# Pacing the row gathers of a mixture-of-experts kernel behind its first-layer results

## The chip, the cores and the metric

The kernel runs on one core of one Trainium2 chip. The metric is the device time of one execution, in microseconds. Engines are called as the profile calls them: PE is TensorE (the matrix engine, PEld its weight loads), DVE is VectorE, ACT is ScalarE, POOL is GpSimd, SP is SyncE. POOL also issues the indirect DMAs, which fetch or store rows by a list of row numbers.

## The reference

Attention over channels gives 20224 tokens of 256 numbers; each token then goes to one of eight experts, with a fixed capacity, best logits first; each expert is a two-layer network.

```python
def _attn_ref(q, k, v, tau):            # B, N, C = 4, 5056, 256
    qn = q / (np.linalg.norm(q, axis=1, keepdims=True) + 1e-06)
    kn = k / (np.linalg.norm(k, axis=1, keepdims=True) + 1e-06)
    s = kn.transpose(0, 2, 1) @ qn / tau
    s = s - s.max(-1, keepdims=True)
    a = np.exp(s)
    a /= a.sum(-1, keepdims=True) + 1e-09
    return (v @ a).astype(np.float32)

def _moe_ref(x, w_gate, w1, w2):        # N, D, E, F = 20224, 256, 8, 1024
    cap = N // E
    order = np.argsort(-(x @ w_gate).flatten())
    for idx in order:                   # greedy: best logits first
        tok, e = (int(idx) // E, int(idx) % E)
        if assigned[tok] >= 0 or counts[e] >= cap:
            continue
        assigned[tok] = e
        counts[e] += 1
...
    for e in range(E):
        mask = assigned == e
        h = np.maximum(x[mask] @ w1[e], 0.0)
        out[mask] = h @ w2[e]
    return out
```

## The kernel before

The first part (to about 340 us) computes the attention and writes its rows x to a table in device memory, x_d. The rest is the expert part, which the change touches. It runs in eight phases p, one expert each. Which tokens the expert gets is found by a routing search on DVE, with small matmuls on PE (L508 and L521 fill pc; DVE answers in Dm and Ex, L511 and L517), which runs one phase ahead beside the matmuls. It ends in a list of row numbers per expert (src to gather, idx to scatter).

An expert's 2528 tokens stand in 20 columns of up to 128, cut into chunks (p, c) of up to four columns: five chunks of 4, or for the first expert 2, 4, 4, 4, 4 and 2. A chunk goes through these steps:

- **Gather** (`load_x`, L1002): per column one indirect DMA on POOL's queue, 128 rows of 1 KB from x_d to the buffer xg, of which there are three. `load_x` only puts the gathers into a Python list, `queue`; `gather()` issues the next one from it. It is called after every unit of layer 1 and every column of layer 2. The gathers of chunk c + 3 are put into the list when chunk c has been turned.
- **Turn** (`turn`, kb = 0 and 1, L1029): PE transposes half the channels of up to four columns into the PSUM buffer pt, ACT copies them to xH (L1031), DVE takes the rest in xL (L1034).
- **Layer 1** (`layer1`): eight units fb, each of six matmuls (L1064: two halves, times the pairs of a high and a low part) into one of three PSUM buffers ph; ACT writes hH with the Relu (L1067), DVE writes hL (L1072). hH and hL have two buffers each, so a chunk's are written again two chunks later.
- **Layer 2** (`layer2`): per column 24 matmuls (L1095) into py, ACT copies to y (L1100), POOL writes one element of `spacer` (L1101) and issues the scatter of the 128 rows to the output (L1102).

Each expert's two weight arrays come by two indirect DMAs from POOL as well (`load_w`, L972); ACT and DVE split them (L981, L984).

The order on PE, ACT and DVE is written down while the program is built: an object `o` keeps a planned clock for PE and DVE, and places DVE's pending work and the routing steps among the matmuls by it. Each engine then works through its own list in order and waits by semaphore for what it needs. POOL's list is the order of the calls. Nothing in the old order ties a gather to PE's or ACT's progress, other than a free xg buffer and the eighth last indirect DMA having landed.

At the start of the expert part six gathers (chunks 0 and 1 of the first phase) are issued at once, those of chunk 2 are in the list, and chunk 3's are added before the first layer 1. The steps are then: turn of chunk 0, layer 1 of chunk 0, turn of chunk 1, layer 2 of chunk 0, layer 1 of chunk 1, in which chunk 2 is turned (first half ahead of unit 2, second half ahead of unit 7), and so on, with layer 1 of a chunk ahead of layer 2 of the one before.

Of the kernel before, what the change touches and what calls it, by code (L numbers as in the profile page):

```python
# [8 lines left out]
F32 = mybir.dt.float32  # L9
# [72 lines left out]
def attention_moe(ctx: ExitStack, tc: tile.TileContext, q, k, vt, tau, wg, w1t, w2t, tabs, out):  # L82
# [3 lines left out]
    P = nc.gpsimd  # L86
# [341 lines left out]
    rt = ctx.enter_context(tc.tile_pool(name="rt", bufs=1))  # L428
# [395 lines left out]
        r["idx"] = idx  # L824
        done["out", p] = True

    spacer = rt.tile([1, 1], F32, name="spacer")
    ge = rt.tile([128, COLS // CG, J, CG], BF, name="ge")
    P.memset(ge, 0.0)
    routed = {}  # L830
# [123 lines left out]
    def n_of(p, c):  # L954
        return sum(n_in(col) for col in cols_of(p, c))
# [3 lines left out]
    def settle():  # L959
        for e in list(pend):  # L960
            if done.get(e[0]):
                pend.remove(e)
                e[1]()
# [40 lines left out]
                in_offset=bass.IndirectOffsetOnAxis(ap=idx[:n, col:col + 1], axis=0)))  # L1004
        xgs[p, c] = xg

    def gather():
        if queue:
            queue.pop(0)()

    queue = []
# [33 lines left out]
    def layer1(p, c, inserts):  # L1045
        o.flush(turned[0])
        xH, xL = xts[p, c]
        nt = n_of(p, c)
        wH, wL = wt[p, 0]
        hH = ffx.tile([128, 8, 512], F32R, name="hH")  # L1050
        hL = ffx.tile([128, 8, 512], F32R, name="hL")
        for fb in range(8):
            for fn in inserts.get(fb, ()):
                fn()
            unit[0] += 1
            phs.append(unit[0])
            if len(phs) > DEPTH:
                o.flush(phs[-1 - DEPTH])
            ph = ps_1.tile([128, 512], F32, name="ph")
            i = 0  # L1060
            for kb in range(2):
                w = slice(kb * F + fb * 128, kb * F + (fb + 1) * 128)
                for l, x_ in ((wH, xH), (wH, xL), (wL, xH)):
                    PE.matmul(ph[:, 0:nt], lhsT=l[:, w], rhs=x_[:, kb, 0:nt], start=(i == 0), stop=(i == 5))  # L1064
                    i += 1
                    o.tick(nt / 2.4 + 3)
            S.activation(hH[:, fb, 0:nt], ph[:, 0:nt], AF.Relu)  # L1067

            lows[p, c] = unit[0]

            def low(ph=ph, fb=fb):
                V.scalar_tensor_tensor(hL[:, fb, 0:nt], ph[:, 0:nt], 0.0, hH[:, fb, 0:nt].bitcast(F32),  # L1072
                                       op0=OP.max, op1=OP.subtract)
            o.post(o.pe + LAYER_LAT, 605, low, phs[-1])
            settle()
            gather()
        return hH, hL

    def layer2(p, c, h, inserts):
        hH, hL = h  # L1080
        o.flush(lows[p, c])
        wH, wL = wt[p, 1]
        o.until(("out", p))
        idx = routed[p]["idx"]
        for i, col in enumerate(cols_of(p, c)):
            for fn in inserts.get(i, ()):
                fn()
            n = n_in(col)
            tk = slice(i * 128, i * 128 + n)
            py = ps_2.tile([128, 512], F32, name="py")  # L1090
            j = 0
            for fb in range(8):
                d = slice(fb * C, (fb + 1) * C)
                for l, w in ((hH, wH), (hH, wL), (hL, wH)):
                    PE.matmul(py[:n, 0:C], lhsT=l[:, fb, tk], rhs=w[:, d], start=(j == 0), stop=(j == 23))  # L1095
                    j += 1
                    if j % 2 == 0:
                        o.tick(2 * 109)
            y = ffx.tile([128, C], F32, name="y", bufs=6)
            S.activation(y[:n], py[:n, 0:C], AF.Copy)  # L1100
            P.memset(spacer, 0.0)  # L1101
            sd = P.indirect_dma_start(out=out, out_offset=bass.IndirectOffsetOnAxis(ap=idx[:n, col:col + 1], axis=0),  # L1102
                                      in_=y[:n], in_offset=None)
            for s_ in scat:
                tc.declare_no_dep(sd.ins, s_.ins, reason="each token is written once")
            scat.append(sd)
            settle()
            gather()

    with tc.manual_schedule():  # L1110
        o.dve = FIRST_LAT
        plan()
        cut_w = [None]

        def first_w():
            load_w(0)
            cut_w[0] = [o.pe + LOAD_LAT] + list(SPLIT)

        want(("ei", 0), first_w)
        for i, (b, c) in enumerate(TODO):  # L1120
            xs = vp.tile([128, T, GW], F32, name="xs", bufs=2)
            for t in range(0, T, 2):
                x_tiles(b, c, t, xs, C, o.tick)
                settle()
                if cut_w[0] and o.pe > cut_w[0][0] and len(cut_w[0]) > 1:
                    split_piece(0, *cut_w[0].pop(1))
                if i + 1 == len(TODO) and t > 0:
                    store_x(b, c, xs, {2: 0, 4: 4, 6: 6}[t], t + 2)
            if i + 1 < len(TODO):
                store_x(b, c, xs)  # L1130
        o.until(("ei", 0))
        settle()
        o.until(("idx", 0))
        actx.close()
        cctx.close()
        ffx = ctx.enter_context(tc.tile_pool(name="ffx", bufs=2))
        ffx.tile([128, PAD_X], F32, name="pad_x", bufs=1)
        ps_1 = ctx.enter_context(tc.tile_pool(name="ps_1", bufs=3, space=PSUM))
        ps_2 = ctx.enter_context(tc.tile_pool(name="ps_2", bufs=2, space=PSUM))
        ps_t = ctx.enter_context(tc.tile_pool(name="ps_t", bufs=1, space=PSUM))  # L1140
        o.margin = MARGIN
        for c in range(2):
            load_x(0, c)
            while queue:
                gather()
        load_x(0, 2)
        for i, q_, eng in cut_w[0][1:]:
            split_piece(0, i, q_, eng)
        idle = ps_1.tile([128, 512], F32, name="ph")
        for i in range(START_TICKS):  # L1150
            o.tick(200)
            PE.matmul(idle, lhsT=wt[0, 0][0][:, 0:128], rhs=wt[0, 0][0][:, 512:1024], start=(i == 0),
                      stop=(i == START_TICKS - 1))
        turn(0, 0, 0)
        turn(0, 0, 1)
        for p in range(E):
            last = p == E - 1
            def turn_at(c, kb):
                return lambda: turn(p, c, kb)

            turns = [] if last else [0, 1]

            def next_turn(force=False):
                if not turns:
                    return
                if force:
                    o.until(("idx", p + 1))
                    settle()
                    while queue:
                        gather()  # L1170
                    while o.pe < routed[p + 1]["time"] + GATHER_LAT:
                        o.tick(100)
                if done.get(("idx", p + 1)) and o.pe >= routed[p + 1]["time"] + GATHER_LAT:
                    turn(p + 1, 0, turns.pop(0))

            if not last:
                want(("ei", p + 1), lambda p=p: load_w(p + 1))
            nchunk = len(cuts[p])
            h = {}
            pieces = {} if p == 0 else {at: [lambda q_=q_: split_piece(p, 1, q_, None)] for q_, at in enumerate((1, 3, 4, 6))}  # L1180
            h[0] = layer1(p, 0, {**pieces} if p == 0 else {2: [turn_at(1, 0)], 7: [turn_at(1, 1)], **pieces})
            for c in range(1, nchunk):
                if p == 0 and c == 1:
                    turn(p, 1, 0)
                    turn(p, 1, 1)
                    layer2(p, 0, h[0], {})
                    h[1] = layer1(p, 1, {2: [turn_at(2, 0)], 7: [turn_at(2, 1)]})
                    continue
                h[c] = layer1(p, c, {})
                ins = {}  # L1190
                if c + 1 < nchunk:
                    for at, kb in ((0, 0), (3, 1)):
                        ins.setdefault(min(at, cuts[p][c - 1] - 1), []).append(turn_at(c + 1, kb))
                elif not last:
                    def w1(p=p):
                        o.until(("ei", p + 1))
                        settle()
                        g = split_w(p + 1, 0, V)
                        for _ in g:
                            o.dve += 600  # L1200
                    ins = {min(1, cuts[p][c - 1] - 1): [w1]}
                layer2(p, c - 1, h[c - 1], ins)
            layer2(p, nchunk - 1, h[nchunk - 1], {i: [next_turn] for i in range(1, 4)})
            while turns:
                next_turn(True)
# [63 lines left out]
```

## Time and profile before

| | us |
|---|---|
| median of 3 runs (lowest, highest) | 1352.06 (1350.59, 1352.67) |
| the profiled execution, its own time | 1351.25 |
| its span in the trace | 1349.5 |
| PE busy in the span | 1308.7 |
| PE matmuls of layer 1 (L1064, xH and xL) | 416.6 and 255.7 |
| PE matmuls of layer 2 (L1095, hH and hL) | 469.0 and 360.0 |
| POOL: 160 scatters, 160 gathers | 161.8, 157.5 |

The span is what the profiler records from the first instruction to the last; 1.75 us of the execution lie around it. Matmuls overlap in the array, so their busy times add up to more than PE's. A line of the profile names an instruction by its line in the kernel, its engine and out<-in by the program's names. An engine's idle time before an instruction is put down to what ended it: another engine's instruction, a DMA, "issue" (nothing that the profile shows) or "remote" (an update whose sender is not seen).

### The profile page before, as it was taken

The page shows a single profiled execution, that of the slowest core. Times are in us where ns is not written, and L with a number is a line of the kernel's source. Part 1 is how long each engine was busy: PE and PEld are TensorE (multiplying, and loading weights), DVE is VectorE, ACT ScalarE, POOL GpSimd, SP SyncE. Part 2 cuts the span into 40 slices and gives each one's busy share as a digit, 9 for nine tenths or more (in the row PEclk, how much of TensorE's full clock was granted, in tenths as well). Part 3 has the DMA queues.
Part 4 walks back from the last instruction along what each step waited for, and adds up shares of the span by engine and source line. Part 5 has one row for each costly group of instructions (what it writes and reads, how often), then busy time and mean ns, then how long its engine had stood idle before and what let it go on. Part 6 is the DMA issues. An engine that isn't in the chain of part 4 may idle for free.

```text
span 1349.5 us, 22880 instructions
## 1 busy us (share of the span) xinstructions
PE 1308.7 (97%) x9162; PEld 1160.4 (86%) x9162; DVE 760.7 (56%) x1912; ACT 527.8 (39%) x1189; POOL 361.6 (27%) x526
## 2 busy tenths in 40 slices
PE   8989999999699999999999999999999999999998
PEld 6877877888589888898899789989898998999998
DVE  5755395768368658767767667674433324233321
ACT  5554452235134334434424423444543334333321
POOL 0000000000422343144333323333434233434122
PEclk9999999999899999999999999999999999999999
DMA  8999884245212122022111311131122113111000
GB/s 282 383 356 345 281 272 156 96 139 201 88 31 87 45 65 93 21 64 99 54 36 47 105 32 44 41 104 44 51 70 82 39 48 108 49 46 57 17 32 31
DMA packets 53706, 143.14 MB, mean 106 GB/s; under 512 B 7776, under 2 KB 28640, under 8 KB 48992
## 3 DMA queue, kind: packets, MB, share of 16 engines
q1 hardware_dynamic: 14544, 62.40, 13.3%
q0 software_dynamic: 17664, 58.22, 13.0%
q10 hardware_dynamic: 21392, 21.06, 4.6%
q8 instruction: 72, 1.18, 0.4%
q14 instruction: 34, 0.28, 0.1%
HBM read 99.97 MB, written 41.68 MB: 105 GB/s over the span
## 4 chain that ended last, share of the span: by engine, by line
PE 72%; issue 12%; DMA 5%; POOL 5%; DVE 3%; another core or an unknown queue 1%; ACT 1%; SPq 0%; POOLq 0%; ACTq 0%
PE py L1095 25%; PE ph L1064 24%; PE px L208 9%; PE s L250 7%; POOL out_dram L1102 3%; DMA ua<-in_q_dram 3%; DMA x_d<-xs 2%; PE pc L508 2%; POOL xg L1002 2%; PE pt L1029 1%; PE px L354 1%; PE pi L717 1%; DVE hL L1072 0%; PE pc L521 0%
## 5 line engine op out<-in xcount | busy, mean ns | idle before, releaser
L1095 PE MATMUL py<-ua,hH 128*128 128x256 f32 (+1 forms) x2560 | 469.0, 283 | 0.0
L1064 PE MATMUL ph<-xH,ua 128*128 128x512 f32 (+3 forms) x1312 | 416.6, 390 | 13.2 <-DVE hL L1072 12.3
L1095 PEld LDWEIGHTS py<-ua,hH 128*128 128x128 f32 (+1 forms) x2560 | 391.2, 187 | 0.4
L1095 PE MATMUL py<-ua,hL 128*128 128x256 f32 (+1 forms) x1280 | 360.0, 281 | 0.0
L1072 DVE SCALAR_TENSOR_TENSOR hL<-ph,hH 128x512 fp32r<-128x512 f32 (+3 forms) x328 | 219.0, 669 | 178.5 <-ACT hH L1067 140.1
L1102 POOL DMA_INDIRECT out_dram<-y,idx x160 | 161.8, 1011 | 530.9 <-ACT y L1100 498.4
L1064 PEld LDWEIGHTS ph<-xH,ua 128*128 128x128 f32 x1312 | 245.9, 190 | 60.5 <-DVE hL L1072 15.3
L1067 ACT ACTIVATE hH<-ph 128x512 fp32r<-128x512 f32 (+3 forms) x328 | 190.4, 583 | 254.2 <-PE ph L1064 206.9
L1064 PE MATMUL ph<-xL,ua 128*128 128x512 f32 (+3 forms) x656 | 255.7, 390 | 0.5 <-DVE xL L1034 0.2
L1095 PEld LDWEIGHTS py<-ua,hL 128*128 128x128 f32 (+1 forms) x1280 | 239.2, 187 | 0.2 <-issue 0.2
L1100 ACT ACTIVATE y<-py 128x256 f32<-128x256 f32 (+1 forms) x160 | 61.5, 385 | 337.0 <-PE py L1095 284.0
L1002 POOL DMA_INDIRECT xg<-x_d,src x160 | 157.5, 984 | 126.5 <-issue 52.9
L250 PE MATMUL s<-ua 128*128 128x256 f32 (+1 forms) x640 | 147.5, 391 | 10.6 <-DMA ua<-in_q_dram 10.6
L250 PEld LDWEIGHTS s<-ua 128*128 128x128 f32 (+1 forms) x640 | 124.9, 197 | 31.6 <-issue 9.9
L1064 PEld LDWEIGHTS ph<-xL,ua 128*128 128x128 f32 x656 | 124.9, 190 | 21.4 <-DVE xL L1034 0.5
L1034 DVE TENSOR_TENSOR xL<-pt,xH 128x512 fp32r<-128x512 f32 (+3 forms) x82 | 54.6, 666 | 121.5 <-ACT xH L1031 120.7
L208 PE MATMUL px<-a,vr 128*128 128x256 f32 (+1 forms) x448 | 104.9, 389 | 2.5 <-ACT xs L212 2.4
L258 ACT ACTIVATE sq<-ua 128x1024 f32<-128x1024 f32 (+1 forms) x72 | 75.7, 1056 | 56.6 <-DMA ua<-in_k_dram 24.4
L208 PEld LDWEIGHTS px<-a,vr 128*128 128x128 f32 x448 | 83.5, 192 | 14.8 <-ACT xs L212 3.1
L212 ACT ACTIVATE xs<-px 128x512 f32<-128x512 f32 (+1 forms) x96 | 49.9, 528 | 91.3 <-PE px L208 88.7
L511 DVE TENSOR_TENSOR Dm<-pc,dmask 128x64 f32<-128x64 f32 (+3 forms) x63 | 12.8, 203 | 97.3 <-PE pc L508 57.4
L774 ACT ACTIVATE junk<-pi,rhalf 128x160 bf16<-128x160 f32 x140 | 54.2, 393 | 24.0 <-PE pi L717 22.0
(275 smaller groups left out, 1104.9 us busy)
## 6 DMA issues: line engine op xcount, KB each, us to landing
x_d<-xs ACTq DMA_DIRECT2D x19, 1024.0 KB, 4.6
ua<-in_k_dram SPq DMA_DIRECT2D x31, 512.0 KB, 6.2
ua<-in_q_dram SPq DMA_DIRECT2D x31, 512.0 KB, 7.5
vr<-in_vt_dram SPq DMA_DIRECT2D x14, 1024.0 KB, 11.7
ua<-in_vt_dram SPq DMA_DIRECT2D x4, 1024.0 KB, 4.7
ua<-in_k_dram SPq DMA_DIRECT2D x8, 480.0 KB, 6.1
ua<-in_q_dram SPq DMA_DIRECT2D x8, 480.0 KB, 7.5
xg<-x_d,src POOLq DMA_INDIRECT x160
```

The source lines that it names most:

```text
L208: mm = PE.matmul(px[:, i * C:i * C + width], lhsT=vs[b, c][:, kb, t + i, :], rhs=a_f[b][:, kb, 0:width], start=(kb == 0), stop=(kb == 1))
L250: newest[0] = PE.matmul(sb[:, ib * C:(ib + 1) * C], lhsT=kt[:np_, t, ib * 128:(ib + 1) * 128], rhs=qt[:np_, t, :], start=(first and t == 0 ...
L258: S.activation(sq[:np_], t_[:np_], AF.Square)
L774: S.activation(junk, pi[:, i * W:i * W + COLS], AF.Sign, bias=rhalf[:, g0 + i:g0 + i + 1], scale=-1.0, accum_out=sgn[:, g0 + i:g0 + i + 1])
L1002: queue.append(lambda i=i, col=col, n=n_in(col): P.indirect_dma_start(out=xg[:n, i, :], out_offset=None, in_=x_d, in_offset=bass.IndirectO ...
L1034: V.tensor_tensor(xL[:, kb, 0:nt], pt[:, 0:nt], xH[:, kb, 0:nt].bitcast(F32), op=OP.subtract)
L1064: PE.matmul(ph[:, 0:nt], lhsT=l[:, w], rhs=x_[:, kb, 0:nt], start=(i == 0), stop=(i == 5))
L1067: S.activation(hH[:, fb, 0:nt], ph[:, 0:nt], AF.Relu)
L1072: V.scalar_tensor_tensor(hL[:, fb, 0:nt], ph[:, 0:nt], 0.0, hH[:, fb, 0:nt].bitcast(F32), op0=OP.max, op1=OP.subtract)
L1095: PE.matmul(py[:n, 0:C], lhsT=l[:, fb, tk], rhs=w[:, d], start=(j == 0), stop=(j == 23))
L1100: S.activation(y[:n], py[:n, 0:C], AF.Copy)
L1102: sd = P.indirect_dma_start(out=out, out_offset=bass.IndirectOffsetOnAxis(ap=idx[:n, col:col + 1], axis=0), in_=y[:n], in_offset=None)
```

## The change

A gather in layer 1 is now issued only after every second unit (fb 1, 3, 5, 7), or after each unit as long as more than four gathers are in the list; in the very first layer 1 only after its last unit. Ahead of each such gather POOL copies one element of that unit's hH into a spare element of `spacer`, so that POOL's list stands until ACT has written that unit. Gathers after a column of layer 2 are issued as before, without a copy. The first half of the third chunk's turn moves from ahead of unit 2 to ahead of unit 4. There are 116 copies.

```diff
-    spacer = rt.tile([1, 1], F32, name="spacer")
+    spacer = rt.tile([1, 2], F32, name="spacer")
+    pace = spacer[:, 1:2]
...
-    def gather():
+    def gather(behind=None):
         if queue:
+            if behind is not None:
+                P.tensor_copy(pace, behind.bitcast(F32))
             queue.pop(0)()
...
             o.post(o.pe + LAYER_LAT, 605, low, phs[-1])
             settle()
-            gather()
+            if fb == 7 or (fb % 2 == 1 or len(queue) > 4) and (p, c) != (0, 0):
+                gather(hH[0:1, fb, 0:1])
         return hH, hL
...
-            P.memset(spacer, 0.0)
+            P.memset(spacer[:, 0:1], 0.0)
...
-                    h[1] = layer1(p, 1, {2: [turn_at(2, 0)], 7: [turn_at(2, 1)]})
+                    h[1] = layer1(p, 1, {4: [turn_at(2, 0)], 7: [turn_at(2, 1)]})
```

POOL's list at the start of the expert part, from the first gather on. The buffers xg_2613, xg_2616, xg_2621 and xg_2700 are those of the first four chunks; x_d_66 is x_d. Before:

```order
L1002 DMA xg_2613<-x_d_66,src_2448 128x256 x2
L1002 DMA xg_2616<-x_d_66,src_2448 128x256 x4
L1002 DMA xg_2621<-x_d_66,src_2448 128x256 x4
L1002 DMA xg_2700<-x_d_66,src_2448 128x256 x4
L1101 MEMSET spacer_1542 1x1
L1102 DMA out_0_dram<-y_2860,idx_2480 20224x256
```

And now, where hH_2702 is the first chunk's layer-1 result and hH_2895 the second's:

```order
L1003 DMA xg_2613<-x_d_66,src_2448 128x256 x2
L1003 DMA xg_2616<-x_d_66,src_2448 128x256 x4
L1011 COPY spacer_1542<-hH_2702 1x1
L1003 DMA xg_2621<-x_d_66,src_2448 128x256
L1105 MEMSET spacer_1542 1x1
L1106 DMA out_0_dram<-y_2854,idx_2480 20224x256
L1003 DMA xg_2621<-x_d_66,src_2448 128x256
L1105 MEMSET spacer_1542 1x1
L1106 DMA out_0_dram<-y_2890,idx_2480 20224x256
L1003 DMA xg_2621<-x_d_66,src_2448 128x256
L1011 COPY spacer_1542<-hH_2895 1x1
L1003 DMA xg_2621<-x_d_66,src_2448 128x256
```

Fourteen gathers in a row have become six. The third chunk's four stand behind the last unit of the first layer 1, behind each of the first chunk's two scatters, and behind the first unit of the second chunk's layer 1; the fourth chunk's follow them.

ACT's list from the first chunk's last y on, with the second chunk's layer 1 (hH) and the third chunk's turn (xH); before:

```order
L1100 ACTIVATE y_2896<-py_2865 128x256
L1067 ACTIVATE hH_2901<-ph_2903 128x512
L1067 ACTIVATE hH_2901<-ph_2937 128x512
L1031 ACTIVATE xH_2952<-pt_2954 128x512
L1067 ACTIVATE hH_2901<-ph_2962 128x512
```

And now:

```order
L1104 ACTIVATE y_2890<-py_2859 128x256
L1070 ACTIVATE hH_2895<-ph_2897 128x512
L1070 ACTIVATE hH_2895<-ph_2932 128x512
L1070 ACTIVATE hH_2895<-ph_2948 128x512
L1070 ACTIVATE hH_2895<-ph_2964 128x512
L1034 ACTIVATE xH_2976<-pt_2978 128x512
```

The first half of the turn stands two units later, on PE and DVE as well; the second half stays ahead of unit 7.

POOL's list around the two loads of the fifth expert's weights (issued at 753 and 763 us in the trace of before), which have gathers behind them, as at four other places; before:

```order
L972 DMA ub0_8049<-in_w1t_dram,ei_7574 128x2048
L972 DMA ub1_8050<-in_w2t_dram,ei_7574 128x2048
L1002 DMA xg_7934<-x_d_66,src_6774 128x256 x2
L1002 DMA xg_8206<-x_d_66,src_6774 128x256 x3
L1002 DMA xg_8206<-x_d_66,src_6774 96x256
```

And now, where hH_8103 and hH_8271 belong to the two chunks in whose layer 1 these gathers are issued:

```order
L973 DMA ub0_8099<-in_w1t_dram,ei_7622 128x2048
L973 DMA ub1_8100<-in_w2t_dram,ei_7622 128x2048
L1011 COPY spacer_1542<-hH_8103 1x1
L1003 DMA xg_7984<-x_d_66,src_6815 128x256
L1011 COPY spacer_1542<-hH_8103 1x1
L1003 DMA xg_7984<-x_d_66,src_6815 128x256
L1011 COPY spacer_1542<-hH_8103 1x1
L1003 DMA xg_8258<-x_d_66,src_6815 128x256
L1011 COPY spacer_1542<-hH_8271 1x1
L1003 DMA xg_8258<-x_d_66,src_6815 128x256
```

Each of the six gathers behind the loads has a copy of its own ahead of it, three of one chunk's units and three of the next one's.

## Prediction

> **What bounds the kernel.** I read the page first, then PE's waits from 345 us on (the expert part), then each engine's timeline where those waits lie. On the page one engine carries the span:
>
> ```profile
> PE 1308.7 (97%) x9162; PEld 1160.4 (86%) x9162; DVE 760.7 (56%) x1912; ACT 527.8 (39%) x1189; POOL 361.6 (27%) x526
> ```
>
> PE is busy 97% of it, so an edit on POOL can pay only where PE stands or runs slowly. PE's waits in the expert part (line waited for: us in total, times, longest):
>
> ```profile
> PE ph L1064 <- DVE hL L1072: 12.3, 7, 9.2
> PE pc L521 <- DVE Ex L517: 3.0, 3, 2.4
> ```
>
> One wait of 9.2 us makes most of the first row, one of 2.4 us most of the second. Both lie beside dense row gathers. The first is in the first chunk's layer 1, here on PE, ACT, DVE and POOL (start, duration, engine, line; in brackets the idle time before and its releaser):
>
> ```profile
> 349.84 0.35 PE L1064 MATMUL ph<-xH,ua 128*128 128x256 f32 x1
> ...
> 351.88 0.40 PE L1064 MATMUL ph<-xH,ua 128*128 128x256 f32 x2
> 352.12 0.28 PE L1064 MATMUL ph<-xL,ua 128*128 128x256 f32 x1
> 352.24 0.40 PE L1064 MATMUL ph<-xH,ua 128*128 128x256 f32 x2
> 352.48 0.76 PE L508 MATMUL pc<-oh,ge 128*128 128x64 bf16 x20
> ...
> 365.08 0.58 PE L1064 MATMUL ph<-xH,ua 128*128 128x256 f32 x1 [9.17 <-DVE hL L1072]
> ...
> 369.09 0.62 PE L1029 MATMUL pt<-identr,xg 128*128 128x128 f32 x4
> 364.19 0.94 ACT L1067 ACTIVATE hH<-ph 128x256 fp32r<-128x256 f32 x3 [11.60 <-remote]
> 364.14 0.23 DVE L511 TENSOR_TENSOR Dm<-pc,dmask 128x64 f32<-128x64 f32 x1 [11.10 <-remote]
> 350.88 0.95 POOL L1002 DMA_INDIRECT xg<-x_d,src  x1 [0.30 <-issue]
> 352.13 0.95 POOL L1002 DMA_INDIRECT xg<-x_d,src  x1 [0.31 <-issue]
> ...
> 360.90 0.95 POOL L1002 DMA_INDIRECT xg<-x_d,src  x1 [0.30 <-issue]
> ```
>
> ACT and DVE both stand for 11 us and start again together, at 364.14 to 364.19, though what they wait for, PE's L508 and L1064, is recorded as run from 352.48 on. So PE's results are seen late, and then PE itself stands, since it has used up its three ph buffers. What else is at work is POOL alone: gathers 1.25 us apart (350.88, 352.13), the last one issued until 360.90 + 0.95 = 361.85. The traffic from 344 to 365 us by queue (packets, MB, share of the DMA engines):
>
> ```profile
> q0 software_dynamic: 672, 1.84, 30.0%
> q8 instruction: 1, 0.02, 0.3%
> ```
>
> All but one packet are those of the 14 gathers, which are all that POOL issued there. PE's results appear 364.14 - 361.85 = 2.3 us after the last issue, about when that gather lands. This is my main reading: while a long train of gathers flows, PE's completions come late. By what path, the trace does not say.
>
> **Part 1, the first train: 14 gathers become 6.** The six gathers of the first two chunks still go back to back; the seventh now stands behind the last unit of the first layer 1. What is lost there now: the layer lasts 369.09 - 349.84 = 19.25 us. Its 48 matmuls, at three per 0.36 us (351.88 to 352.24), need 5.8, and L508 in between 0.76, together 6.6. So 12.7 us are lost, part of it to a slow clock, as this window shows (bounds and length, then busy time of PE, PEld, DVE, ACT, POOL, PE's clock, DMA share, GB/s):
>
> ```profile
> 365.00:369.10 4.10, 4.02 (x19) 4.02 (x20) 1.74 (x6) 0.89 (x3) 0.00 (x0) 0.50 0.00 2
> ```
>
> Afterwards the sixth gather is issued until 350.88 + 0.95 = 351.83, and 2.3 us later, at 354.1, the hold ends; L508, done at 352.48 + 0.76 = 353.24, is then seen 0.9 us late. I leave that 0.9 of the loss: -11.8. Ends: -12.7 (no hold at all) and 0 (the train is not the cause); the rows of this very place lie nearest to the first.
>
> The row to weigh is ACT's, 11.60 us of standing beside 672 packets of gathers. [...]
>
> **Part 2, the train behind the weights.** The second long stall, on POOL and DVE, and in windows:
>
> ```profile
> 763.16 0.94 POOL L972 DMA_INDIRECT ub<-in_w2t_dram,ei  x1 [8.79 <-DVE ua L984]
> 764.41 0.95 POOL L1002 DMA_INDIRECT xg<-x_d,src  x1 [0.30 <-issue]
> ...
> 770.68 0.92 POOL L1002 DMA_INDIRECT xg<-x_d,src  x1 [0.31 <-issue]
> 771.59 0.19 DVE L511 TENSOR_TENSOR Dm<-pc,dmask 128x32 f32<-128x32 f32 x1 [3.77 <-remote]
> 769.90:772.30 2.40, 0.05 (x1) 0.00 (x0) 0.71 (x6) 0.00 (x0) 1.49 (x3) 1.00 0.34 104
> 772.30:775.40 3.10, 3.06 (x8) 2.48 (x9) 2.33 (x11) 1.39 (x3) 0.00 (x0) 0.50 0.11 32
> 1012.00:1026.00 14.00, 14.00 (x66) 11.57 (x65) 8.03 (x13) 6.99 (x12) 6.70 (x8) 1.00 0.40 130
> ```
>
> Six gathers pile up behind the second weight load, which waits 8.79 us for DVE. PE loses 2.40 standing and half of 3.10 at half clock: 3.9. In the new order two or three of the six still follow at once, because their units are done when the load is released; the rest come one per two units. The last row is a like place, a weight load and six gathers, and there PE is busy 14.00 of 14.00: such a train does not always cost. Ends 0 and -3.9; with as much train left as taken away I take half, -2.0.
>
> **Part 3, smaller trains.** Two windows, with the same columns:
>
> ```profile
> 466.30:479.00 12.70, 10.62 (x91) 10.04 (x90) 3.90 (x11) 2.53 (x7) 9.69 (x12) 0.87 0.33 102
> 498.00:506.00 8.00, 7.36 (x52) 5.66 (x52) 5.05 (x11) 3.75 (x8) 4.38 (x5) 1.00 0.27 79
> ```
>
> In the first, the queue holds more than four gathers and the units are short (224 tokens), so the new rule still issues one per unit and the train stays: 0. What that place loses now is 12.70 - 10.62 = 2.1 idle and, at a mean clock of 0.87, (0.13/0.50) x 12.7 = 3.3 us at half speed, so 1.65 more: 3.7 in all, for eight gathers. In the second PE is idle 0.64; those gathers are paced at two units, so I take -0.6. Ends: 0 and -(3.7 + 0.6) = -4.3.
>
> **Part 4, the third chunk.** Its four gathers were in the first train; now the fourth waits for the first unit of the second chunk's layer 1. That place before (PE, ACT, POOL), and the landing of one gather from the chain of waits:
>
> ```profile
> 377.23 0.39 PE L1064 MATMUL ph<-xH,ua 128*128 128x512 f32 x1
> 380.89 0.46 PE L1029 MATMUL pt<-identr,xg 128*128 128x128 f32 x4
> 380.25 0.60 ACT L1067 ACTIVATE hH<-ph 128x512 fp32r<-128x512 f32 x1 [2.44 <-PE ph L1064]
> 378.09 1.00 POOL L1102 DMA_INDIRECT out_dram<-y,idx  x1 [0.45 <-issue]
> 345.65 2.55 DMA xg<-x_d,src
> ```
>
> Counted from that layer's first matmul (377.23): POOL's scatter of the first chunk ends at +1.86, the third gather follows it and is issued by about +3.1 (1.25 a gather); ACT's first unit ends at +3.62; the copy and an issue gap of 0.3 give about +4.1; landing 2.55 later is +6.65. PE wants it at the turn: +3.66 before, and two units more. A unit is six matmuls of 512 columns at twice the 0.12 us of 256, so 1.44, and the turn comes at +6.54. PE waits 0.1; I take +0.2. Ends: 0, and +3.8 if a result is seen as late here as at 771.59 (3.77). Late next is nothing: the turn's other half comes three units later, its place unchanged. On ACT and DVE the turn's two instructions move with it past two units each; their number and length stay, cost 0.
>
> **Part 5, 116 copies on POOL.** The nearest POOL groups (count, then busy us, mean ns, idle before), and what POOL waits for most:
>
> ```profile
> L1101 POOL MEMSET spacer<- 1x1 f32 x160 | 15.1, 94 | 0.1
> L279 POOL TENSOR_TENSOR nd<-nd,nrm 128x4 f32<-128x4 f32 x4 | 1.9, 466 | 1.2 <-DVE nd L278 1.2
> POOL out_dram L1102 <- ACT y L1100: 498.4, 142, 15.5
> ```
>
> 116 x 94 to 466 ns is 10.9 to 54.1 us, on an engine that stands 498.4 us waiting for y alone. Behind a waiting copy are queued one gather and then scatters, whose y comes from matmuls that PE runs after that unit anyway. Weight loads have no copy between them and the scatter or gather ahead of them. Apart from the third chunk's, the gathers are wanted more than a chunk later. ACT's write of the same hH buffer two chunks on has to wait for the copy, long done by then. Cover: POOL's standing time; cost 0. If copies slow DVE, the upper end is a second time the 3.0 us that PE waits for Ex: +3.0; nothing here gives a gain.
>
> **Sum.** -11.8 - 2.0 - 0.6 + 0.2 + 0 = -14.2. The profiled execution took 1351.25 us: 1337.05. The median of the runs, 1352.06, lies 0.8 above it and gives 1337.9. I say 1337.
>
> **Rivals.** *The train moves (13%).* At the second chunk's layer 1 the queue holds nine, so the gathers go one per unit of 1.44 us, hardly sparser than 1.25. If PE is held there as at 466 to 479, it loses 3.7 us, or twice that for a hold that slows the clock longer: 1341 to 1345. Against it: a gather now needs the unit before it seen as finished, so a held PE stops the train that holds it. *The gathers are not the cause (13%).* Parts 1 and 2 give nothing: 1351.25 - 0.4, between 1350 and 1353, no change. For it: no row names a path, and 1012 to 1026 is a train without loss. Against it: both long stalls end within 2.3 us of a train's end, on two engines at once. [...] *Slower (6%): each gather holds PE by itself*, wherever it stands, and a train hides that by sharing one hold. At 466 to 479 a gather cost 3.7/8 = 0.46 us. With 116 places it decides from 14.2/116 = 0.12 us each; at 0.2 the time is 1337 + 23 = 1360. Against it: the 14.00 of 14.00 above. *More (6%)*: parts 1 to 3 go to their ends, -12.7 - 3.9 - 4.3 = -20.9: 1330.
>
> **How the numbers follow.** My forecast, 1333 to 1341, has 62%. From 1330 to 1348 lie also the first rival, most of the fourth, and a first stall only half removed: about 8 in 10. Left out are the no-cause case and the slower one. A measurement of this kernel tells about 0.2% (2.7 us) from no change: faster 0.81, same 0.13, slower 0.06.
>
> **What would show it.** Right: six gathers in the first train; no 11 us wait of ACT and DVE near 353; the first layer 1 near 7.5 us, with the clock at 1.00 after it; the row of PE waiting for hL near 3 us; at the third chunk PE's transposes wait for xg less than 1 us. Wrong: the 11 us wait stands though six gathers went (not the cause), or it comes back some 15 us later in the second chunk (train moves), or PE shows many short waits behind hL (slower).

## The result, and the profile after

The changed kernel takes 1331.33 us (median of 4 runs, 1329.69 to 1333.54) against 1351.32 for the kernel before (4 runs, 1350.17 to 1352.67): a ratio of 0.9853, with a 95% interval of 0.9834 to 0.9871, 20 us less. The profiled execution took 1331.89 us, its span is 1330.1. The median lies just below my forecast of 1333 to 1341, and inside 1330 to 1348. The experiments below put a limit on this number: on four other occasions, on chips 5, 0, 14 and 9 (the record does not number the chip of this first pair), the kernel before took 1323 us itself, and neither the change (chip 0) nor any variant of it was faster.

First the profile of the changed kernel. Its lines in the code stand one to four further down: the gather is L1003, the copy L1011, the turn L1032, layer 1 L1067 with ACT's L1070 and DVE's L1075, the scatter L1106. The page's first line, and three rows of PE's waits from 345 us on:

```profile
PE 1301.9 (98%) x9162; PEld 1157.0 (87%) x9162; DVE 761.9 (57%) x1912; ACT 528.3 (40%) x1189; POOL 386.9 (29%) x642
PE ph L1067 <- issue: 1.9, 1, 1.9
PE ph L1067 <- DVE hL L1075: 1.4, 3, 0.7
PE pc L521 <- DVE Ex L517: 1.1, 3, 0.5
```

The row of hL fell from 12.3 us to 1.4, its longest wait from 9.2 to 0.7; the row of Ex from 3.0 to 1.1. The first layer 1, on PE, ACT, DVE and POOL:

```profile
348.38 0.35 PE L1067 MATMUL ph<-xH,ua 128*128 128x256 f32 x1
...
351.02 0.76 PE L508 MATMUL pc<-oh,ge 128*128 128x64 bf16 x20
...
355.53 0.46 PE L1032 MATMUL pt<-identr,xg 128*128 128x128 f32 x4
352.13 0.38 ACT L1070 ACTIVATE hH<-ph 128x256 fp32r<-128x256 f32 x1 [1.01 <-PE ph L1067]
351.81 0.22 DVE L511 TENSOR_TENSOR Dm<-pc,dmask 128x64 f32<-128x64 f32 x1 [0.23 <-PE pc L508]
349.39 0.94 POOL L1003 DMA_INDIRECT xg<-x_d,src  x1 [0.30 <-issue]
356.18 0.18 POOL L1011 COPY spacer<-hH 1x1 f32<-1x1 f32 x1 [5.85 <-ACT hH L1070]
```

The last of six gathers is issued by 350.33; L508, started at 351.02, is answered by DVE at 351.81, and the layer lasts 355.53 - 348.38 = 7.15 us instead of 19.25. POOL stands ahead of the copy for 5.85 us until ACT has written the last unit. Windows of the changed kernel (bounds and length, busy time of PE, PEld, DVE, ACT, POOL, PE's clock, DMA share, GB/s): the first layer 1, the place of the eight-gather train that was to stay, and the train behind the fifth expert's second weights:

```profile
348.40:355.50 7.10, 6.97 (x70) 6.53 (x69) 3.75 (x11) 3.07 (x8) 1.62 (x2) 1.00 0.19 59
451.80:466.80 15.00, 12.26 (x107) 11.68 (x105) 7.31 (x22) 3.06 (x10) 10.89 (x17) 0.90 0.25 76
748.90:757.00 8.10, 7.75 (x52) 5.98 (x51) 6.01 (x23) 2.99 (x5) 5.86 (x10) 1.00 0.55 196
```

PE is at work 6.97 of 7.10 us at full clock in the first. The second still loses 15.00 - 12.26 = 2.74 standing, and at a mean clock of 0.90 another (0.10/0.50) x 15 / 2 = 1.5; here gathers still go one per 224-token unit, and the wait that the page puts down to "issue" lies in this place:

```profile
462.84 0.37 PE L1067 MATMUL ph<-xH,ua 128*128 128x224 f32 x1 [1.85 <-issue]
458.81 0.98 POOL L1003 DMA_INDIRECT xg<-x_d,src  x1 [0.16 <-issue]
460.13 0.97 POOL L1003 DMA_INDIRECT xg<-x_d,src  x1 [0.16 <-issue]
```

The third loses 0.35. To see where the 20 us come from, the table gives the time from the first gather to the first layer-2 matmul of every fifth group of 96, in the traces of both kernels (the two columns at the right are explained below):

| from the first gather to | before | after | before_again | after_again |
|---|---|---|---|---|
| layer 2, matmul 1 | 27.1 | 14.9 | 14.9 | 16.2 |
| matmul 481 | 178.3 | 166.3 | 159.5 | 160.8 |
| matmul 961 | 305.2 | 292.4 | 285.2 | 286.5 |
| matmul 1441 | 435.3 | 419.1 | 410.5 | 411.8 |
| matmul 1921 | 563.8 | 545.9 | 537.0 | 538.3 |
| end of the span | 1005.1 | 987.2 | 978.3 | 979.6 |

From before to after 12.2 us are gained up to the first row, none to the second, 0.8 to the third, 3.4 to the fourth, 1.8 to the fifth, nothing later: 17.9 in all. The other 1.5 of the 19.4 us between the two spans lie ahead of the expert part, where the kernels are alike (first gather at 344.39 and 342.90).

### The profile page after: what moved, and what is told of

Same layout as the page of the kernel before. It is cut to its first block, busy times and chain, and to the rows that moved or that the text cites. A ratio compares the mean times of both kernels' runs of the same rounds, so it can differ in the third digit from the quotient of the medians.

```text
span 1330.1 us, 23080 instructions
## 1 busy us (share of the span) xinstructions
PE 1301.9 (98%) x9162; PEld 1157.0 (87%) x9162; DVE 761.9 (57%) x1912; ACT 528.3 (40%) x1189; POOL 386.9 (29%) x642
## 4 chain that ended last, share of the span: by engine, by line
PE 55%; issue 5%; POOL 2%; DVE 1%; ACT 0%; POOLq 0%
PE ph L1067 26%; PE py L1099 25%; PE pc L508 2%; PE pt L1032 1%; POOL out_dram L1106 1%; PE pi L717 1%; PE pc L521 0%; POOL spacer L1105 0%; DVE m L464 0%; DVE f L489 0%; DVE xL L1037 0%; POOLq L1268 0%; ACT hH L1070 0%; DVE eq L486 0%; DVE L L683 0%
## 5 line engine op out<-in xcount | busy, mean ns | idle before, releaser
L1067 PE MATMUL ph<-xH,ua 128*128 128x512 f32 (+3 forms) x1312 | 412.5, 388 | 3.3 <-issue 1.9
L1075 DVE SCALAR_TENSOR_TENSOR hL<-ph,hH 128x512 fp32r<-128x512 f32 (+3 forms) x328 | 219.3, 670 | 171.6 <-ACT hH L1070 140.4
L1067 PEld LDWEIGHTS ph<-xH,ua 128*128 128x128 f32 x1312 | 243.3, 188 | 48.7 <-DVE hL L1075 3.0
L1070 ACT ACTIVATE hH<-ph 128x512 fp32r<-128x512 f32 (+3 forms) x328 | 190.9, 583 | 232.2 <-PE ph L1067 208.9
L1106 POOL DMA_INDIRECT out_dram<-y,idx x160 | 159.7, 998 | 398.7 <-ACT y L1104 364.9
L1067 PE MATMUL ph<-xL,ua 128*128 128x512 f32 (+3 forms) x656 | 253.9, 387 | 0.3 <-DVE xL L1037 0.2
L1003 POOL DMA_INDIRECT xg<-x_d,src x160 | 161.0, 1006 | 97.7 <-issue 48.4
L1067 PEld LDWEIGHTS ph<-xL,ua 128*128 128x128 f32 x656 | 123.4, 188 | 21.4 <-DVE xL L1037 0.5
L774 ACT ACTIVATE junk<-pi,rhalf 128x160 bf16<-128x160 f32 x140 | 54.1, 392 | 24.0 <-PE pi L717 22.0
L511 DVE TENSOR_TENSOR Dm<-pc,dmask 128x64 f32<-128x64 f32 (+3 forms) x63 | 12.8, 202 | 83.0 <-PE pc L508 59.1
```

The lines of the kernel that those rows point to most:

```text
L774: S.activation(junk, pi[:, i * W:i * W + COLS], AF.Sign, bias=rhalf[:, g0 + i:g0 + i + 1], scale=-1.0, accum_out=sgn[:, g0 + i:g0 + i + 1])
L1003: queue.append(lambda i=i, col=col, n=n_in(col): P.indirect_dma_start(out=xg[:n, i, :], out_offset=None, in_=x_d, in_offset=bass.IndirectO ...
```

## The experiments

My theory was the prediction's: a long train of gathers makes PE's completions late. The first rivals were that the gain is the pacing of everything later, that the copies (the tie to ACT) are what helps, and that it takes a fetch of PE's instruction code inside a train (the trace of before has 72 such fetches, packets of 16,384 B on q8, with 256 of PE's instructions from one to the next on average). Beside each experiment the kernel before ran on the same chip, and the ratios are to that.

**start_only**, chip 5: only the first layer 1 is changed.

```diff
-            if fb == 7 or (fb % 2 == 1 or len(queue) > 4) and (p, c) != (0, 0):
-                gather(hH[0:1, fb, 0:1])
+            if (p, c) != (0, 0):
+                gather()
+            elif fb == 7:
+                gather(hH[0:1, fb, 0:1])
```

> Only the first layer 1 is changed as in the change (no gather at units 0 to 6, one behind a copy at unit 7; the third chunk's turn at unit 4); everything later is issued as before, one gather per unit without a copy. If the length of the first train is what held PE, the 11.6 us wait of ACT and DVE is gone and the time is about 12 us under before, 1339 (1337 to 1341), with the stalls near 770 us as before. If the gain came from pacing everywhere else, 1349 to 1352. If the first hold only moves into the second chunk's layer 1, 1341 to 1348.

Measured: 1323.73 us, and the kernel before on that chip 1323.13 (31 runs, 1321.02 to 1327.73); ratio 1.0002 (0.9993 to 1.0012). No expectation was for that: there was no hold to take away.

**no_first**, chip 5: everything but the first layer 1.

```diff
-            if fb == 7 or (fb % 2 == 1 or len(queue) > 4) and (p, c) != (0, 0):
+            if (p, c) == (0, 0):
+                gather()
+            elif fb % 2 == 1 or len(queue) > 4:
                 gather(hH[0:1, fb, 0:1])
...
-                    h[1] = layer1(p, 1, {4: [turn_at(2, 0)], 7: [turn_at(2, 1)]})
+                    h[1] = layer1(p, 1, {2: [turn_at(2, 0)], 7: [turn_at(2, 1)]})
```

> The change without its rule for the first layer 1, whose gathers follow one per unit without a copy (a train of 14 again), and with the third chunk's turn back at unit 2; all later gathers are paced as in the change. If the first train's length is the cause, the 11 us hold stands, and what is left is the later part of the gain, 5 to 7 us: 1344 to 1347. If the hold belongs to something else that the change moved, below 1340.

Measured: 1323.37, ratio 1.0008 (0.9997 to 1.0018). It has a first train of 14 gathers, as the kernel before, and PE's waits from 345 us on are these:

```profile
PE pt L1032 <- DVE xL L1037: 2.2, 2, 1.3
PE pt L1032 <- DMA xg<-x_d,src: 0.7, 1, 0.7
PE ph L1067 <- DVE hL L1075: 0.5, 1, 0.5
```

The same train, and a longest wait for hL of 0.5 us instead of 9.2. So a train of 14 does not by itself hold PE.

**no_copies**, chip 5: the change's places, without the copies.

```diff
-                gather(hH[0:1, fb, 0:1])
+                gather()
```

> The change's places for the gathers, without the copies: the first train has seven gathers, later ones come four in a row behind a chunk's scatters. If it is the number of gathers in a row at the start that holds PE, seven behave nearly as six: 1331 to 1341. If the copies (the tie to ACT's progress) are needed for the gain, 1345 to 1352. If the copies themselves cost time, below 1330.

Measured: 1323.17, ratio 0.9996 (0.9985 to 1.0007). Neither the copies nor the places count where there is no hold.

**shift_before**, chip 5: the kernel before with its idle matmuls ahead of the first turn cut finer.

```diff
-        for i in range(START_TICKS):
-            o.tick(200)
+        for i in range(4 * START_TICKS):
+            o.tick(50)
...
-            PE.matmul(idle, lhsT=wt[0, 0][0][:, 0:128], rhs=wt[0, 0][0][:, 512:1024], start=(i == 0),
-                      stop=(i == START_TICKS - 1))
+            PE.matmul(idle[:, 0:128], lhsT=wt[0, 0][0][:, 0:128], rhs=wt[0, 0][0][:, 512:640], start=(i == 0),
+                      stop=(i == 4 * START_TICKS - 1))
```

> The kernel before, with the 24 idle matmuls of 512 columns ahead of the first turn cut into 96 of 128: the same columns, 144 more PE instructions. PE's instructions arrive in fetches of 16 KB, 256 instructions; in the kernel before one falls inside the first train (353.1 us) and one inside the train at 763 to 771 us (768.4). The shift moves both out of the trains. If the train of gathers alone holds PE, the 11 us hold and the stall near 770 stand: 1350 to 1353. If a fetch that falls into a train is what holds PE, both go: 1334 to 1340, with gathers issued as before.

Measured: 1328.75, ratio 1.0044 (1.0034 to 1.0054), slower for a reason outside the question. The groups of idle matmuls, of shift_before and of before_again:

```profile
L1152 PE MATMUL ph<-ua 128*128 128x128 f32 x96 | 11.2, 275 | 0.7 <-ACT xs L212 0.7
L1152 PE MATMUL ph<-ua 128*128 128x512 f32 x24 | 6.2, 403 | 0.7 <-ACT xs L212 0.7
```

A quarter of the columns does not take a quarter of the time: 11.2 us instead of 6.2, and the first turn comes 5 us later. On the question itself, no_first shows that a fetch inside a train is not enough: one falls into its train (at 350.4 us), and nothing is held; before_again's packets from 342 to 363 us, with its train of 14 in them, hold one too (q8, 0.02 MB), and its longest wait for hL is 0.5 us. Whether a fetch had a part on the first occasion stays open.

**before_again** and **after_again**, chip 0: the two kernels of this document unchanged, for profiles of both from one chip.

> The kernel before once more, for a second profile. In the last four runs, on a chip where the kernel before takes 1323 us, a first train of 14 gathers held nothing. If the hold of PE is a property of the kernel, its profile has the 11 us wait again and the time is 1350 to 1353. If it belongs to the chip or to the recording on it, the profile on a 1323 us chip shows no hold, and all of the 16 updates that each of 336 indirect DMAs gives (5376) are recorded; on a chip of the first kind, where before's profile recorded 3308 and after's 4205, the hold and the missing records come together.

> The changed kernel once more. If the gain is the kernel's own, 20 us under before wherever it runs. If it is only what the change saves of a hold that some chips have, within 2 us of before on a chip without the hold, and 1330 to 1333 on one with it.

Measured: before_again 1322.92, ratio 1.0003 (0.9991 to 1.0015); after_again 1323.55, ratio 0.9999 (0.9988 to 1.0011). In the table above, after_again is 1.3 us behind before_again from the first row on: in the window from 347.40 to 355.30 us, with its first layer 1 from 349.69 on, PE's mean clock is 0.78, and three matmuls take 0.64 us (351.80 to 352.44) instead of 0.36. The same kernel before, the same place as in the prediction's third block of lines:

```profile
347.92 0.35 PE L1064 MATMUL ph<-xH,ua 128*128 128x256 f32 x1
...
350.55 0.76 PE L508 MATMUL pc<-oh,ge 128*128 128x64 bf16 x20
...
355.07 0.45 PE L1029 MATMUL pt<-identr,xg 128*128 128x128 f32 x4
351.67 0.38 ACT L1067 ACTIVATE hH<-ph 128x256 fp32r<-128x256 f32 x1 [1.01 <-PE ph L1064]
351.35 0.22 DVE L511 TENSOR_TENSOR Dm<-pc,dmask 128x64 f32<-128x64 f32 x1 [0.23 <-PE pc L508]
350.14 0.94 POOL L1002 DMA_INDIRECT xg<-x_d,src  x1 [0.30 <-issue]
...
358.88 0.95 POOL L1002 DMA_INDIRECT xg<-x_d,src  x1 [0.30 <-issue]
```

Gathers follow every 1.25 us until 358.88, and the layer takes 355.07 - 347.92 = 7.15 us, to the hundredth what the changed kernel takes. Windows of before_again: the first layer 1, the train of gathers and scatters that cost 3.7 us before, and the train behind the fifth expert's weights:

```profile
347.90:355.10 7.20, 7.07 (x71) 6.63 (x71) 3.81 (x11) 3.07 (x8) 5.42 (x6) 1.00 0.38 113
451.00:464.00 13.00, 13.00 (x131) 12.98 (x130) 7.92 (x22) 6.09 (x15) 10.25 (x12) 1.00 0.34 102
738.00:746.00 8.00, 8.00 (x56) 6.54 (x55) 7.35 (x23) 4.23 (x9) 4.57 (x5) 1.00 0.46 165
```

PE does not stand in any of them, with the DMA engines as busy (0.38, 0.34, 0.46) as where it was held (0.30 to 0.34 in the prediction's rows). So the hold belongs to the occasion, a chip or its state, and not to the kernel alone. What differs in the traces is the record of the semaphore updates. The issue line of the gathers (engine queue, operation, count, median us to landing) in the first pair's before, and in before_again:

```profile
xg<-x_d,src POOLq DMA_INDIRECT x160
xg<-x_d,src POOLq DMA_INDIRECT x160, 2.8
```

The first has no time to landing, because landings are not fully recorded. At 16 updates for each of the 336 indirect DMAs 5376 are due, and before_again has 5351 / 336 = 15.9 for each. Counted in the traces, as updates that a DMA sent: before 3292, after 4189, before_again 5351, after_again 5357 (the 3308 and 4205 in my expectation each hold 16 updates at the end of the run that no DMA sent). In the first pair's before, indirect DMAs with one other within 6 us have 15.6 of their 16 on average, those with five others 5.6; in before_again both have 16.0. The engines' own updates are missing too: of PE's 1082 are recorded where before_again has 1135, of DVE's 1576 of 1664, of ACT's 956 of 1033. Both traces hold the same 22,880 instruction records. So on the first occasion updates are missing where indirect DMAs are dense, and the changed kernel misses fewer.

A lost record is not yet a hold, though. In the first pair's before, ACT starts a unit at 352.20, right behind a matmul that ended at 352.16 and whose update has no record: the update was seen in time. The weight load and six gathers from 1014 to 1022 us, beside which PE was busy 14.00 of 14.00, have 4, 4, 2, 0, 5, 3 and 16 of their 16; the changed kernel's first six gathers have 7, 4, 16, 4, 5 and 16, and no hold follows. In the hold itself PE's updates are not lost but late, and come together: the matmuls that owe the next four end at 353.24, 353.56, 354.28 and 355.91, and the next four updates of PE are recorded at 364.12, 364.16, 364.24 and 364.31, 8.4 to 10.9 us behind. In before_again all but one of PE's 1134 matmuls that give an update have it recorded within 0.06 us of their end.

**plus8**, chip 0: the change, with the long train put back as eight gathers that nobody waits for.

```diff
+        spare = ffx.tile([128, 6, C], F32, name="spare", bufs=1)
+        holds = [spare[:, i, :] for i in range(6)] + [xgs[0, 0][:, i, :] for i in (2, 3)]
+        for i in range(8):
+            P.indirect_dma_start(out=holds[i][:128], out_offset=None, in_=x_d,
+                                 in_offset=bass.IndirectOffsetOnAxis(ap=routed[0]["src"][:128, 2 + i:3 + i], axis=0))
         load_x(0, 2)
```

> The change, with eight more gathers of 128 rows right behind the first six, into spare rows that nobody reads: the long train is back, with nothing waiting for it. If trains hold PE on this chip, the 11 us wait is back and the time is 10 to 14 us over the change's. On a chip without the hold, or if the train is not the cause, it is within 2 us of the change.

Measured: 1324.94, ratio 1.0015 (0.9998 to 1.0032). No hold; PE's longest wait for hL is again this:

```profile
PE ph L1067 <- DVE hL L1075: 0.5, 1, 0.5
```

**flood_small** and **flood_large**, chip 14: many landings with few bytes, and many bytes with few landings, from the changed kernel's sixth gather on. Could more load bring the hold on an occasion without it?

```diff
+        spare = ffx.tile([128, 6, C], F32, name="spare", bufs=1)
+        P.memset(spare[:, 0:3, :], 0.0)
+        for i in range(96):
+            nc.sync.dma_start(spare[:, i // 32, i % 32 * 8:i % 32 * 8 + 8], x_d[i * 128:(i + 1) * 128, 0:8])
```

```diff
+        spare = ffx.tile([128, 6, C], F32, name="spare", bufs=1)
+        P.memset(spare[:, :, 0:1], 0.0)
+        for i in range(10):
+            nc.sync.dma_start(spare[:, i % 2 * 3:i % 2 * 3 + 3, :],
+                              x_d[i * 384:(i + 1) * 384, :].rearrange("(p r) c -> p r c", p=128))
```

> The change, with 96 small DMAs (128 rows of 32 B from x_d into spare elements) on SyncE's queue from the sixth gather on, over the first layer 1: many landings and updates, few bytes. If it is the number of DMA updates, or of their records, that makes PE's completions late, PE is held here on any chip, by 3 to 12 us, and update records go missing in the trace. If the hold needs something that only some chips have, the time is within 2 us of the change's on a chip where the kernel before takes 1323 us, and 3 us or more above it on one where that takes 1351.

> The same place, with ten DMAs of 384 KB from x_d on SyncE's queue: about twice the bytes of the 14 gathers, few landings. If it is the traffic that holds PE, 3 to 12 us over the change. If traffic does not touch PE, within 2 us of the change.

Measured: flood_small 1323.21, ratio 1.0002 (0.9992 to 1.0012); flood_large 1325.15, ratio 1.0014 (1.0004 to 1.0025). The kernel before took 1323.08 there. The load came later than planned: 10 of the 96 small DMAs were issued within the first layer 1 (348.6 to 356.3 us) and the last at 399.4, 4 of the 10 large ones within it (351.6 to 360.6 us) and the last at 370.75. The traces of flood_small and before_again record up to 469 and 172 updates in 10 us of the expert part (the last 30 us left out), the first pair's before at most 108 and after 138. Since records are lost in the first pair, before_again's 172 are the measure of what the kernel asks for: 2.7 times that passes here without holding PE. In the 10 us with the 469 updates PE is at work throughout:

```profile
368.50:378.50 10.00, 10.00 (x68) 8.19 (x67) 8.19 (x19) 4.57 (x8) 6.23 (x10) 1.00 0.44 89
```

PE's longest wait in flood_large, whose trace is of the slowest of its ten runs (1329.84 us), is no hold but a gather that lands late among the traffic; that it makes the 2 us of the median is likely, not shown:

```profile
376.62 0.47 PE L1032 MATMUL pt<-identr,xg 128*128 128x128 f32 x2 [1.97 <-DMA xg<-x_d,src]
```

**plus8_2, start_only_2, flood_small_2**, chip 9: the same three kernels, in the hope of an occasion with the hold.

> The change with eight more gathers behind the first six, once more, in the hope of a chip with the hold (there the kernel before takes 1351 us, the change 1331). If a long train is what brings the hold on such a chip, 1341 to 1346 with the 11 us wait near 353; if the train is not its cause even there, 1331 to 1334. On a chip where the kernel before takes 1323 us, 1323 to 1326 either way.

> Only the first train shortened. On a chip with the hold: about 12 us under before, 1339, if part 1 of the prediction has the size that the profiles gave; 1331 if the start is all of the gain. On a chip without it: the same as before.

> The change with 96 small DMAs over the first layer 1. On a chip with the hold: 3 us or more over the change if many landings and their updates are what holds PE, within 2 us of it if it takes gathers. On a chip without it: the same as before, as on the chip of the last call.

Measured: 1324.09, 1323.76 and 1323.73, ratios 1.0010 (1.0000 to 1.0021), 1.0006 (0.9994 to 1.0017) and 0.9999 (0.9989 to 1.0009), beside 1322.98 for the kernel before. The hold did not come, so these runs do not separate trains from landings where it exists. One of the ten runs of start_only_2 took 4267.54 us; no trace of it was kept, and its cause is not known. Over the four chips the kernel before ran 100 times, between 1321.02 and 1327.73 us. No kernel of these beats it there.

**What stays open** is why the first occasion had the hold. That the updates have a ceiling there is my guess, from some of the counts: a train asks for 16 updates every 1.25 us, 12.8 per us, besides the engines' own, and no 10 us of the first before's expert part record more than 108; a gather every second unit of 1.44 us asks for 5.6. Against it, the same trace records 193 updates in 10 us near its start (from 2.5 us on), and the train at 1014 us loses as many records without a hold. So the ceiling is argued, not shown, and no run of mine met that occasion. Whether the lost records and the late completions have one cause, or whether the recording is that cause, could not be tried either: every run here carries a record.

## Why the prediction was right, and where it was not

**The reading of the bound** (PE, late completions beside dense gathers) held for the occasion that it was read from, and nowhere else. The step that failed is the sentence "while a long train of gathers flows, PE's completions come late", taken as a rule of the chip: no_first, before_again and plus8 have such trains and lose nothing. The prediction had the sign of this in hand, the window 1012 to 1026 with PE busy 14.00 of 14.00, and used it to halve part 2 and in two rivals, not against the reading itself. That the number came near is owed to the occasion: result and first profile come from the one that had the hold, and on the four others the same reading had nothing to remove (after_again 0.9999). On the occasion itself the signs named for being right all came: six gathers, no 11 us wait, a first layer 1 of 7.15 us with the clock at 1.00 after it, 1.4 us of waiting for hL (I had named 3), and part 4's wait below.

**Part 1** (-11.8, ends -12.7 and 0): measured -12.2, table's first row. The layer took 7.15 us where 7.5 was forecast, and the 0.9 us left for L508 did not come (0.23 us of DVE's wait).

**Part 2** (-2.0, ends 0 and -3.9): measured -3.4, table's fourth row. Halving was the wrong choice; a train of a weight load and four gathers (748.90 to 757.00) lost 0.35 us, not half of the 3.9.

**Part 3** (466 to 479 stays; 498 to 506 -0.6): the eight-gather train stayed and loses 4.2 us (2.74 and 1.5) against 3.7. In the place of 498 to 506 (now 484 to 493) PE stands 9.00 - 8.78 = 0.22 us instead of 0.64. Not in the sum at all were 0.8 us up to the table's third row and 1.8 in the fifth, though the ends (to -4.3) had room for them; in the fifth PE stood 128.50 - 127.71 = 0.79 us before (779.7 to 908.2) and not at all after.

**Part 4** (+0.2): PE waited 0.35 us for the fourth gather of the third chunk.

```profile
370.61 0.28 PE L1032 MATMUL pt<-identr,xg 128*128 128x128 f32 x1 [0.35 <-DMA xg<-x_d,src]
```

**Part 5** (116 copies, 0): the group took 24.3 us of POOL, within the 10.9 to 54.1 worked out.

```profile
L1011 POOL COPY spacer<-hH 1x1 f32<-1x1 f32 x116 | 24.3, 210 | 117.8 <-ACT hH L1070 102.3 <-DVE mxs L528 8.0 <-issue 4.3
```

Of 117.8 us of standing before it, 102.3 wait for ACT's hH. That it costs nothing is shown by after_again (0.9999) and no_copies (0.9996).

**The sum** of -14.2 came out as -17.9 in the expert part. Part 1 gave 12.2 of it, so parts 2 to 4 gave 5.7 where 2.4 was forecast, 3.3 too little; the rest of the 19.4 us between the spans, 1.5, lies ahead of the expert part and is not the change's.

**The rivals.** The train did not move: in the second chunk's layer 1 gathers go one per unit, and the time from the table's first row to its second is 151.4 us, against 151.2 before. "Each gather holds PE by itself" fell too, with 116 copies and no loss. Of the rivals' times, 1330 for *More* is nearest to the 1331.33 measured: parts 1 and 2 nearly reached their ends. "The gathers are not the cause" is the one to look at again. On the first occasion the rows speak against it: ACT's 11.60 us are gone with the train. On the four others its result, no change, is what was measured. There PE was busy 7.07 of 7.20 us beside a DMA share of 0.38 (before_again). In the first pair ACT stood 11.60 us beside gathers; what it waited for there were PE's updates, which came up to 10.9 us late.

## What to carry to other kernels

A stall that only one profile shows is a fact about that occasion: before it becomes a mechanism, run the same kernel on another chip, and ask of the trace whether its own records are complete there (here 3292 of 5376). Dense trains of indirect DMAs cost nothing on four chips (with shorter ones no_copies, after_again, flood_small and flood_small_2 took 0.9996, 0.9999, 1.0002 and 0.9999 of the time of the kernel before), and lie beside most of the 27 us that the first occasion lost (12.7, 3.9, 3.7 and 0.6 in the windows that the prediction reads); tying the gathers to results that come just in time cost nothing on the four chips either (after_again 0.9999, no_first 1.0008, flood_small 1.0002, flood_small_2 0.9999; on the first occasion no run has the copies apart), so it may be cheap insurance, and is no speed-up there. And where a window in the same profile shows the suspected cause without its effect, that window deserves more weight than half a term.

## What the hardware showed that I had not expected

The same instructions, with nearly the same busy times (DVE 760.7 and 763.0 us, ACT 527.8 and 528.4), take 1351 us on one occasion and 1323 on four others, and 26.8 of the 28.8 us between the spans of 1349.5 and 1320.7 lie in the expert part (1005.1 against 978.3 from the first gather), most of it in places where indirect DMAs are dense and their updates go unrecorded (73 of the 224 that the first train's 14 gathers owe are recorded from 344 to 365 us). In the longest of these places four updates of PE came up to 10.9 us late and within 0.2 us of one another, while DMA landings went on being recorded (19 updates of them from 355.92 to 364.12 us). And 96 matmuls of 128 columns took 11.2 us of PE where 24 of 512 took 6.2: the same columns at 1.8 times the cost.
